# Splitting the attention output products by output rows

## The chip, the cores and the metric

The kernel runs on one core of a Trainium2 chip. The metric is the device time of one execution in microseconds. Three executions of the kernel before took 728.78, 730.17 and 731.63 us; the median is 730.17 us.

## The reference

An attention-like recurrence over 768 steps feeds two gated feed-forward stages. For 4 batches and 8 heads with a head dimension of 40:

```python
for t in range(S):
    m_new = np.maximum(f_gate[:, :, t] + m, i_gate[:, :, t])
    f_stab = np.exp(f_gate[:, :, t] + m - m_new)
    i_stab = np.exp(i_gate[:, :, t] - m_new)
    C = f_stab * C + i_stab * einsum('bhd,bhe->bhde', vt, kt)
    n = f_stab * n + i_stab * kt
    y[:, :, t] = sigmoid(o_gate_t) * (C @ qt) / max(|n . qt|, 1)
x = y.transpose(0, 2, 1, 3).reshape(3072, 320)
x = ((x @ w1) * (x @ w2)) @ w3 @ w_out
out = max(x @ v1, x @ v2, x @ v3) @ v_out
```

(The state `C`, `n` is broadcast over its two inner dimensions in the source; the lines are shortened here. The second stage's weights, which the source also calls w1 to w_out, are called v here.)

## The kernel before

**Attention in units.** The 768 steps are cut into 9 chunks: 8 of 88 steps and a last one of 64. With 4 batches and 2 groups of 4 heads that makes 72 units, numbered `u`; `ub(u)` (called at the head of each function) gives batch `b`, chunk `c`, head group `g`, the chunk's length `n` and the number `r` of rows that the products contract over (88 in the first chunk, 128 in the others, where the rows above 88 carry the state of the chunks before).

A unit has two products on TensorE. The score product (`L569` for units up to 27, four float32 products with 40 rows; `L594` for the later ones, four with 120 rows) gives `s`. VectorE multiplies it by the decay matrix `dd` into `pk` (`L610`), GpSimd writes the columns of `pk` that build the next state (`L559`). Then `outs(u)` forms the output product: for each of 4 heads, `pk` is the stationary operand and the 41 columns of `kv` (values and a column of ones) are the moving one. Its output has 128 rows: rows 0 to 87 are this chunk's outputs, the others are state for the unit `u + 2`. In the last chunk nothing follows, so there the stationary operand has only 64 columns.

`rest(u)` follows on VectorE and GpSimd: the state goes into `kv` of unit `u + 2` (`L630`), the outputs are divided by their denominators (`L643` to `L646`) and gated (`L651`). `x_cols` transposes the result (`L666`) into the feed-forward stages.

**A product in float32 is two passes.** Each `PE.matmul` on float32 operands leaves two weight loads and two matmuls in the trace: one `outs` is 4 products, or 8 passes. The products of the feed-forward stages use rounded operands (`F32R`) and are one pass each.

**Feed-forward.** `a_step` and `c_step` run groups of 8 matmuls with 128 stationary and 384 moving columns (`L698` to `L702`); `b_step` (`L765` to `L769`) and `d_step` (`L784`) accumulate; `fold` (`L926`) multiplies two weight matrices ahead of time.

**What sets the order.** A planner (`Plan.run`) simulates the engines with fixed costs and due times shifted by a table (`BIAS`) and writes out one order of instructions per engine. The cost that it is told for `outs` is a constant in the call of `P.op` (910 or 500 ns; 1210 ns together with the score product), and so the order doesn't depend on how `outs` is written. For units `u >= DUO = 28` the output product of unit `u - 1` stands in the same step as the score product of unit `u`, straight behind it. So the outputs of units 27 to 70 follow `L594`; those of units 0 to 26 and of unit 71 stand where the planner put them. Units 0 to 9 write `o` into the banks `ac0` to `ac2`, the later ones into `aq`.

Of the kernel before, what the change touches and what calls it, by code (L numbers as in the profile page):

```python
# [280 lines left out]
def mlstm_moe_kernel(  # L281
# [21 lines left out]
    V, A, G, PE, SP = nc.vector, nc.scalar, nc.gpsimd, nc.tensor, nc.sync  # L303
# [33 lines left out]
    o, where, over, gates_done = 0, {}, {t: [] for t, _ in shared}, {}  # L337
# [30 lines left out]
    def T(*key):  # L368
        return made[key]
# [7 lines left out]
    o = 0  # L377
# [30 lines left out]
    def f():  # L408
# [5 lines left out]
         r=[("g", "ff")], w=[("g", "git")])  # L414

    def f():
# [6 lines left out]
         r=[("g", "git")], w=[("g", "aug", 1)])  # L423
# [55 lines left out]
    def ub(u):  # L479
        b, r = divmod(u, 18)  # L480
        return b, r // 2, r % 2, GL[r // 2], 128 if r > 1 else L
# [41 lines left out]
    def unit(u):  # L523
# [48 lines left out]
        else:  # L572
# [19 lines left out]
            def f():  # L592
                for h in range(4):
                    PE.matmul(T("s", u)[0:L, h], lhsT=ks[:, h], rhs=T("qs", u)[:, h], start=True, stop=True)  # L594
                if duo:
                    outs(u - 1)
# [19 lines left out]
        if u + 1 < DUO or u == NU - 1:  # L616
            new(("o", u), [128, 4, 41], F32, f"ac{u % 3}" if u < 10 else "aq")
            P.op("P", 910 if m > n else 500, lambda: outs(u), cols=210, r=[("pk", u), ("kv", u)], w=[("o", u)])
            rest(u)

    def outs(u):
        b, c, g, n, r = ub(u)
        m = 128 if c < NCH - 1 else n
        for h in range(4):
            PE.matmul(T("o", u)[:m, h], lhsT=T("pk", u)[:r, h, 0:m], rhs=T("kv", u)[:r, h, 40:81], start=True, stop=True)  # L625

    def rest(u):
        b, c, g, n, r = ub(u)
# [514 lines left out]
```

## Time and profile before

| | |
|---|---|
| median of three executions | 730.17 us (728.78 to 731.63) |
| profiled execution: span from its first to its last instruction | 729.3 us (the page gives no other time for it) |
| instructions | 12666 |
| TensorE matmul (PE) busy | 699.4 us, 96%, 4341 instructions |
| TensorE weight load (PEld) busy | 674.3 us, 92%, 4341 instructions |
| VectorE (DVE) busy | 437.0 us, 60% |
| ScalarE (ACT) busy | 373.8 us, 51% |
| GpSimd (POOL) busy | 308.3 us, 42% |
| mean granted TensorE clock | 0.988 of full speed |

Matmuls are pipelined and their ends are modelled, so the time of one row is longer than the distance to the next; what TensorE really takes is read from the starts of successive rows. A row of the timeline merges neighbouring instructions of one line: start, length from the first start to the last end, and their number. `128*64` in a row is the part of the TensorE array that is used: rows times columns of the stationary operand.

### The profile page before, as it was taken

The page shows a single profiled execution, that of the slowest core. Times are in us where ns is not written, and L with a number is a line of the kernel's source. Part 1 is how long each engine was busy: PE and PEld are TensorE (multiplying, and loading weights), DVE is VectorE, ACT ScalarE, POOL GpSimd, SP SyncE. Part 2 cuts the span into 40 slices and gives each one's busy share as a digit, 9 for nine tenths or more (in the row PEclk, how much of TensorE's full clock was granted, in tenths as well). Part 3 has the DMA queues.
Part 4 walks back from the last instruction along what each step waited for, and adds up shares of the span by engine and source line. Part 5 has one row for each costly group of instructions (what it writes and reads, how often), then busy time and mean ns, then how long its engine had stood idle before and what let it go on. Part 6 is the DMA issues. An engine that isn't in the chain of part 4 may idle for free.

```text
span 729.3 us, 12666 instructions
## 1 busy us (share of the span) xinstructions
PE 699.4 (96%) x4341; PEld 674.3 (92%) x4341; DVE 437.0 (60%) x998; ACT 373.8 (51%) x697; POOL 308.3 (42%) x438
## 2 busy tenths in 40 slices
PE   1699999999999999999999999999999999999998
PEld 1677897889999999999999999999999999999998
DVE  4688876667766865866466676754747632233333
ACT  5968998689854355555343446545333222231311
POOL 1786755556646536664044456543406200000000
PEclk9978999999999999999999999999999999999999
DMA  7987887464433445543023445432305100000000
GB/s 207 251 247 226 233 230 219 146 185 157 148 88 102 117 111 148 139 124 87 12 76 85 109 121 153 113 83 69 88 1 112 49 1 27 1 1 1 1 27 28
DMA packets 50954, 78.84 MB, mean 108 GB/s; under 512 B 11882, under 2 KB 37930, under 8 KB 50890
## 3 DMA queue, kind: packets, MB, share of 16 engines
q1 hardware_dynamic: 50890, 78.04, 38.4%
q8 instruction: 34, 0.56, 0.3%
q14 instruction: 30, 0.25, 0.1%
HBM read 73.98 MB, written 4.03 MB: 107 GB/s over the span
## 4 chain that ended last, share of the span: by engine, by line
PE 84%; DMA 7%; DVE 3%; POOL 2%; issue 2%; SPq 1%; ACT 0%; POOLq 0%; DVEq 0%
PE wk L698 13%; PE wk L699 12%; PE wk L700 12%; PE ac L784 9%; PE aq L625 6%; PE wk L702 6%; PE wk L701 6%; PE ac L765 4%; PE ac L769 4%; PE wk L926 4%; PE ac L767 3%; DMA stg<-in_w3t 2%; PE aq L569 2%; PE aq L594 1%; DMA dd<-d_na 1%
## 5 line engine op out<-in xcount | busy, mean ns | idle before, releaser
L718 DVE TENSOR_TENSOR pl<-pr,ph 128x384 fp32r<-128x384 f32 (+1 forms) x91 | 60.8, 669 | 75.8 <-ACT ph L714 73.1
L714 ACT CAST ph<-pr 128x384 fp32r<-128x384 f32 (+1 forms) x114 | 57.8, 510 | 90.5 <-PE ac L784 43.9
L698 PE MATMUL wk<-xh,wch 128*128 128x384 f32 x288 | 99.5, 345 | 0.0
L700 PE MATMUL wk<-xl,wch 128*128 128x384 f32 x288 | 97.1, 337 | 0.0
L699 PE MATMUL wk<-xh,wcl 128*128 128x384 f32 x288 | 97.1, 337 | 0.0
L749 DVE TENSOR_TENSOR pr<-pr,wk 128x384 f32<-128x384 f32 (+1 forms) x98 | 52.8, 541 | 64.4 <-PE wk L702 57.8
L698 PE MATMUL wk<-xh,wah 128*128 128x384 f32 x256 | 90.9, 355 | 0.0
L718 POOL TENSOR_TENSOR pl<-pr,ph 128x384 fp32r<-128x384 f32 (+1 forms) x23 | 24.2, 1052 | 153.7 <-ACT ph L714 138.9
L699 PE MATMUL wk<-xh,wal 128*128 128x384 f32 x256 | 86.6, 338 | 0.0
L700 PE MATMUL wk<-xl,wah 128*128 128x384 f32 x256 | 86.5, 338 | 0.0
L545 POOL TENSOR_TENSOR dd<-am,dd 128x352 f32<-128x352 f32 (+2 forms) x72 | 57.5, 799 | 49.6 <-DMA dd<-d_na 48.8
L559 POOL TENSOR_TENSOR pk<-kv,dd 128x160 f32<-128x160 f32 (+1 forms) x64 | 38.7, 606 | 72.1 <-PE aq L625 64.9
L625 PE MATMUL aq<-kv,pk 128*128 128x41 f32 (+2 forms) x496 | 62.2, 275 | 2.1 <-POOL pk L559 1.4
L731 ACT COPY pr<-wk 128x384 f32<-128x384 f32 x64 | 30.5, 477 | 64.2 <-PE wk L702 64.1
L553 ACT ACTIVATE dd<-dd 128x352 f32<-128x352 f32 (+2 forms) x72 | 35.2, 492 | 52.3 <-POOL dd L549 51.7
L625 PEld LDWEIGHTS aq<-kv,pk 128*128 128x128 f32 (+2 forms) x496 | 57.4, 184 | 4.5 <-POOL pk L559 1.7
L651 POOL TENSOR_TENSOR misc<-misc 88x160 f32<-88x160 f32 (+1 forms) x62 | 41.5, 669 | 46.7 <-DVE misc L646 42.5
L746 ACT COPY pr<-wk 128x384 f32<-128x384 f32 x48 | 23.1, 482 | 70.5 <-PE wk L702 70.4
L733 DVE TENSOR_TENSOR pr<-pr,wk 128x384 f32<-128x384 f32 x64 | 35.2, 551 | 40.0 <-PE wk L702 35.7
L698 PEld LDWEIGHTS wk<-xh,wch 128*128 128x128 f32 x288 | 54.1, 188 | 0.1
L699 PEld LDWEIGHTS wk<-xh,wcl 128*128 128x128 f32 x288 | 54.2, 188 | 0.0
L700 PEld LDWEIGHTS wk<-xl,wch 128*128 128x128 f32 x288 | 54.0, 188 | 0.0
(133 smaller groups left out, 1729.5 us busy)
## 6 DMA issues: line engine op xcount, KB each, us to landing
misc<-in_qk SPq DMA_DIRECT2D x44, 330.0 KB
dd<-d_na SPq DMA_DIRECT2D x56, 176.0 KB
kv<-in_kv SPq DMA_DIRECT2D x72, 121.5 KB
stg<-in_w3t SPq DMA_DIRECT2D x13, 512.0 KB
stg<-in_wc SPq DMA_DIRECT2D x9, 512.0 KB
qq<-in_qk SPq DMA_DIRECT2D x64, 66.0 KB
misc<-in_og SPq DMA_DIRECT2D x31, 120.0 KB
out<-misc SPq DMA_DIRECT2D x23, 160.0 KB
```

The source lines that it names most:

```text
L545: P.op("G", 735, lambda: G.tensor_tensor(out=T("dd", u)[:r], in0=am[:r, c, h0:h0 + 4].unsqueeze(2).to_broadcast([r, 4, n]), in1=T("dd", u) ...
L625: PE.matmul(T("o", u)[:m, h], lhsT=T("pk", u)[:r, h, 0:m], rhs=T("kv", u)[:r, h, 40:81], start=True, stop=True)
L651: P.op("G", 485, lambda: G.tensor_tensor(out=yv(), in0=yv(), in1=sg(b, c).rearrange("p (h d) -> p h d", d=D)[:n, g * 4:g * 4 + 4], op=ALU.mult
L698: PE.matmul(p, lhsT=h_[:, kt], rhs=xh[:, kt], start=kt == 0, stop=False)
L699: PE.matmul(p, lhsT=l_[:, kt], rhs=xh[:, kt], start=False, stop=False)
L700: PE.matmul(p, lhsT=h_[:, kt], rhs=xl[:, kt], start=False, stop=False)
L701: PE.matmul(p, lhsT=r_, rhs=xh[:, 2], start=False, stop=False)
L702: PE.matmul(p, lhsT=r_, rhs=xl[:, 2], start=False, stop=True)
L714: P.op("A", act(n), lambda sl=sl: A.copy(out=T("ph", key)[:, sl], in_=T(*src)[:, sl]), r=[src + part], w=[("ph", key) + part])
L718: e.tensor_tensor(out=T("pl", key)[:, sl], in0=T(*src)[:, sl], in1=T("ph", key)[:, sl].bitcast(F32), op=ALU.subtract)
L749: P.op("V", dve(sl.stop - sl.start), lambda ps=ps, sl=sl: V.tensor_tensor(out=T(*sc)[:, sl], in0=T(*sc)[:, sl], in1=T(*ps)[:, sl], op=ALU. ...
L784: PE.matmul(T(f"ac{m}", (k, 1)), lhsT=src[:, m * 128:m * 128 + 128], rhs=w[:, o:o + DM], start=first_, stop=last_,)
```

## The change

In `outs`, each product whose stationary operand has 128 columns is written as two products of 64 columns. The first writes output rows 0 to 63, the second rows 64 to 127. Both have the same moving operand. Where the operand has 64 columns already (the last chunk), there is still one product. Nothing else changes; the planner gets the same costs, and so the order of the work is the same.

```diff
     def outs(u):
         b, c, g, n, r = ub(u)
         m = 128 if c < NCH - 1 else n
         for h in range(4):
-            PE.matmul(T("o", u)[:m, h], lhsT=T("pk", u)[:r, h, 0:m], rhs=T("kv", u)[:r, h, 40:81], start=True, stop=True)
+            for a in range(0, m, 64):
+                PE.matmul(
+                    T("o", u)[a:a + 64, h], lhsT=T("pk", u)[:r, h, a:a + 64], rhs=T("kv", u)[:r, h, 40:81],
+                    start=True, stop=True,
+                )
```

## Rows read from the trace of the kernel before

**Rows 1.** Page, busy us (share of the span) and instructions of each engine.
```profile
PE 699.4 (96%) x4341; PEld 674.3 (92%) x4341; DVE 437.0 (60%) x998; ACT 373.8 (51%) x697; POOL 308.3 (42%) x438
```

**Rows 2.** Page, the chain that ended last, share of the span by engine.
```profile
PE 84%; DMA 7%; DVE 3%; POOL 2%; issue 2%; SPq 1%; ACT 0%; POOLq 0%; DVEq 0%
```

**Rows 3.** Busy time by stretch: length, each engine's busy us (instructions), clock, DMA.
```profile
100.00:225.00 125.00, 124.22 (x755) 112.86 (x754) 86.66 (x193) 100.95 (x169) 69.51 (x89) 1.00 0.55 163
225.00:600.00 375.00, 374.33 (x2444) 371.06 (x2443) 235.50 (x566) 161.68 (x342) 170.77 (x250) 1.00 0.34 91
```

**Rows 4.** Groups by shape, L625: count, busy us, mean ns, idle before.
```profile
L625 PE MATMUL aq<-kv,pk 128*128 128x41 f32 x384 | 50.5, 281 | 2.1 <-POOL pk L559 1.4 <-DVE xl L680 0.6
...
L625 PE MATMUL aq<-kv,pk 128*64 128x41 f32 x64 | 5.3, 233 | 0.0
```

**Rows 5.** Groups by shape, weight loads of L625.
```profile
L625 PEld LDWEIGHTS aq<-kv,pk 128*128 128x128 f32 x384 | 47.3, 192 | 3.3 <-POOL pk L559 1.7 <-DVE xl L680 1.0
...
L625 PEld LDWEIGHTS aq<-kv,pk 128*64 128x64 f32 x64 | 4.3, 137 | 1.0 <-issue 0.7
```

**Rows 6.** Timeline, PE, a 128-column unit behind L594 (start us, us, what).
```profile
405.10 0.44 PE L594 MATMUL aq<-qs,kst 120*88 120x88 f32 x4
405.37 1.06 PE L625 MATMUL aq<-kv,pk 128*128 128x41 f32 x8
406.26 0.42 PE L698 MATMUL wk<-xh,wch 128*128 128x384 f32 x1
...
406.69 0.34 PE L700 MATMUL wk<-xl,wch 128*128 128x384 f32 x1
```

**Rows 7.** Timeline, PE, a 64-column unit behind L594.
```profile
435.16 0.44 PE L594 MATMUL aq<-qs,kst 120*88 120x88 f32 x4
435.53 0.66 PE L625 MATMUL aq<-kv,pk 128*64 128x41 f32 x8
436.12 0.44 PE L698 MATMUL wk<-xh,wah 128*128 128x384 f32 x1
...
436.57 0.34 PE L700 MATMUL wk<-xl,wah 128*128 128x384 f32 x1
```

**Rows 8.** Timeline, PE, a 128-column unit behind a 384-column matmul.
```profile
206.48 0.34 PE L702 MATMUL wk<-xl,wcr 128*128 128x384 f32 x1
206.65 0.98 PE L625 MATMUL aq<-kv,pk 128*128 128x41 f32 x8
207.46 0.42 PE L698 MATMUL wk<-xh,wch 128*128 128x384 f32 x1
...
207.89 0.34 PE L700 MATMUL wk<-xl,wch 128*128 128x384 f32 x1
```

**Rows 9.** Timeline, PE, a 64-column unit behind a 384-column matmul.
```profile
590.39 0.34 PE L702 MATMUL wk<-xl,war 128*128 128x384 f32 x1
590.66 0.66 PE L625 MATMUL aq<-kv,pk 128*64 128x41 f32 x8
591.25 0.45 PE L698 MATMUL wk<-xh,wah 128*128 128x384 f32 x1
...
591.71 0.34 PE L700 MATMUL wk<-xl,wah 128*128 128x384 f32 x1
```

**Rows 10.** Timeline, PE, a unit behind the 40-row score products of L569.
```profile
75.30 0.71 PE L569 MATMUL aq<-misc 40*88 40x88 f32 x7
75.94 1.09 PE L625 MATMUL aq<-kv,pk 128*128 128x41 f32 x8
```

**Rows 11.** Waits of PE: who waited for whom, us in total, times, longest.
```profile
PE aq L569 <- DMA raw<-in_qk: 10.3, 2, 8.1
...
PE aq L625 <- POOL pk L559: 1.4, 1, 1.4
```

**Rows 12.** Timeline, PE, a unit of the first 30 us.
```profile
23.87 1.93 PE L625 MATMUL ac<-kv,pk 88*128 88x41 f32 x8
25.73 2.65 PE L569 MATMUL aq<-raw 40*88 40x88 f32 x16
```

## The prediction

> **What bounds the kernel now.** I read the page's busy times first, then the chain that ended last, then busy time by stretch, then the groups by shape, and last the timeline around single units. TensorE is busy 96% of the span with matmuls and 92% with weight loads [rows 1], and 84% of the chain is its own work [rows 2]. The stretch that holds most of the changed work is fuller still: from 100 to 225 us it is busy 124.22 of 125 us, from 225 to 600 us 374.33 of 375 us [rows 3]. Nothing there waits for another engine for long, and VectorE and GpSimd have a third and more of their time free. So in these 500 us, whatever the TensorE queue gains or loses per output product, the end gains or loses. Before that TensorE waits for loads (10.3 us in two waits [rows 11]), and small delays can vanish in such waits.
>
> What bounds a single pass is read from the starts. Eight passes of 128 stationary and 41 moving columns take 1.06 us from the first start to the last end, and one is shown with 281 ns [rows 4, 6]: (1.06 - 0.28) / 7 = 111 ns per step. A unit of the last chunk has the same 41 moving columns and 64 stationary ones: (0.66 - 0.23) / 7 = 61 ns [rows 4, 7], its first, slower step included. The mean weight load is 192 ns against 137 ns, 55 ns less [rows 5], and 111 - 55 = 56. I take 58 ns. Half the stationary columns, about half the step, with the moving side unchanged: the weight load sets the pace, and the load of one pass is hidden by nothing but the matmul of the pass before.
>
> **The change part by part.** *Passes.* Of 72 units, the 8 of the last chunk stay as they are. The other 64 go from 8 passes of 128 columns to 16 of 64. If the loads of the two halves follow one another as all loads do now, that is 16 x 58 = 928 ns in place of 8 x 111 = 888 ns: 40 ns more per unit, 2.6 us in all. On passes alone it would be a change hardly to be seen.
>
> *Going in and out of the 64-column form.* The units of the last chunk are a model of what a split unit does, for they stand between the same neighbours and use 64 columns. They don't gain what their shorter steps promise. Behind `L594`, the distance from the first score pass to the third feed-forward matmul is 406.69 - 405.10 = 1.59 us with 128 columns [rows 6] and 436.57 - 435.16 = 1.41 us with 64 [rows 7]: 0.18 us saved, where 8 x 53 ns = 0.42 us should have been. The other 0.24 us stands at the two edges: 0.37 us from `L594` to the first output pass in place of 0.27, and 436.12 - 435.53 = 0.59 us until `L698` starts, where eight steps of 58 make 0.46. The same behind a 384-column matmul: 1.41 us [rows 8] against 1.32 us [rows 9], 0.09 saved of 0.42, so 0.33 us at the edges; there a load that ran under the long matmul is lost as well. These are prices of this kernel's own instructions; I take it that they hang on the 64 columns and not on the chunk.
>
> A split unit is then a last-chunk unit with eight further passes of 58 ns (0.47 us):
> - Behind `L594`: 1.41 + 0.47 - 1.59 = +0.29 us. The units are 27 to 70 without the five of the last chunk among them: 39, so +11.3 us.
> - Behind a 384- or 320-column matmul: 1.32 + 0.47 - 1.41 = +0.38 us. These are 11 of the 15 later units that remain: +4.2 us.
> - Behind the 40-row products `L569` (the other 4 of the 15, the first of them in [rows 10]): the unit there takes 1.09 us where it takes 0.98 to 1.06 elsewhere, so it pays an entry already. I charge half of the 0.24 us and the passes: +0.17 us each, +0.7 us; bounds 0.04 and 0.29.
> - The ten units of the first 60 us: here a unit takes 25.73 - 23.87 = 1.86 us [rows 12], twice what it takes later, and the neighbours are mostly 40-row products. Bounds 0 and 0.29 us each; I take 0.1, near the lower end because those edges are paid already: +1.0 us.
>
> Sum: 11.3 + 4.2 + 0.7 + 1.0 = +17.2 us.
>
> *What takes some of it back.* The output product waits for GpSimd's part of `pk` once for 1.4 us [rows 11], and twice for VectorE's `xl`, 0.6 us together [rows 4]; a later TensorE finds them shorter. I take 2.2 us off, between 0 and 4 (the two load waits stand too early for much to pile up ahead of them). That leaves +15 us.
>
> *Who waits longer.* Behind an output product stand the state for unit `u + 2` and the division on VectorE, then the gate on GpSimd. They get `o` 0.3 us later, on engines that are not full; I cost this at nothing, and if the chain from state to `pk` to output were tight, TensorE would have idle time in [rows 3]. The 512 further weight loads and matmuls write nothing extra and release nobody earlier: the signal still comes with the last pass. No DMA, no wait and no buffer is added.
>
> The profiled execution had a span of 729.3 us; it would become 744.3. The median of the runs is 0.9 us above that span, so the forecast is 745 us.
>
> **The rivals.** *The two halves load side by side (faster).* They use different columns of the array, so the load of one might run while the other's does. Then eight further passes cost nothing, and a split unit costs what a last-chunk unit costs: -0.18 us behind `L594` (39: -7.0), -0.09 behind long matmuls (11: -1.0), -0.30 behind `L569` (4: -1.2), some -0.5 early: -10 us, 720 us. It decides from the step on: the unit breaks even where 16 passes save 0.29 us, at 58 - 18 = 40 ns per pass. For it: the loads are the bound, and the columns are disjoint. Against it: every load in the trace comes one after another, and nothing before uses the upper 64 columns alone, so no row shows two at once.
> The Trainium skill speaks on both sides. "TensorEngine Tiling (Array Packing)", section Key Properties, says that different tiles of the array can load weights and multiply in parallel; by it this rival holds. "TensorE: Matmul & The Clock Gate", Part 3, The mechanism, says that a weight load overlaps with a running matmul only where the row group differs; the two halves use the same rows, so by it they would gain nothing. The trace already departs from that second rule, since loads overlap with the matmul before them on the same rows (a step of 111 ns holds both), so I don't let it decide.
>
> *Each change between the halves costs as much as an edge (much slower).* If going from rows 0-63 to rows 64-127 costs about half of 0.24 us, seven such changes stand inside each unit: 64 x 7 x 0.12 = 54 us more, 799 us. Nothing in the trace shows a change of columns within one form; the edges are seen where the form changes, and that speaks against it.
>
> *The edges don't apply.* If they belong to the last chunk and not to the 64 columns (or the halves are run in the full form), 40 ns per unit remain: +2.6 us, 733 us. Against it: the edges appear both at [rows 7] and at [rows 9], with different neighbours.
>
> **How the numbers follow.** Loads in sequence with edges: 0.54, 738 to 750 us by itself (0.20 to 0.32 us per unit behind `L594`, 0 to 4 us taken back). Halves side by side: 0.33, 717 to 729, the upper part where they overlap only in part. No edges, or an overlap near break-even: 0.07, 730 to 737. Changes between halves dear: 0.06, from 752. The range from 719 to 750 leaves out the last case and the tails. About 0.5% (3.7 us) is what a measurement can tell from no change. Faster is the rival without its upper end: 0.31. Same takes that end and the bottom of the third case: 0.07. Slower is the rest: 0.62.
>
> **What would show it.** `L625` should have 1088 passes in place of 576, all of 64 columns. A unit behind `L594` should take about 0.9 us from its first to its last start, with 58 ns per step across the change of halves too, and the entry (0.37 us) and the exit of [rows 7] on every unit. If the step across halves is near 30 ns, the first rival holds; if it is 150 ns or more at every second pass, the second. If the units are as forecast but the end moves by less than 10 us, the waits took back more than I allowed. The forecast fails altogether if the unit as a whole, entry to exit, is shorter than 1.59 us.

## The result, and the profile after

The changed kernel takes 723.39 us (median of four, 722.34 to 725.08) against 729.68 us (median of four, 728.78 to 731.63; the first three of them gave 730.17): a ratio of 0.9913, with a 95% interval of 0.9892 to 0.9934, or 6.3 us less. The time lies inside the stated range, near the first rival's 720 us. The forecast was 745 us, 15 us more than before: the direction was wrong.

In the kernel after, the line of the output products is `L626`, and the later lines are four higher (`L698` is `L702`). The page's busy times, to set beside [rows 1]:
```profile
PE 682.0 (94%) x4853; PEld 648.9 (90%) x4853; DVE 437.6 (61%) x998; ACT 373.4 (52%) x697; POOL 306.3 (42%) x438
```
TensorE has 512 more matmuls and as many more weight loads, as expected, and yet 17 us less busy time. The groups by shape say where (line, engine, operation, tiles, shape, count, busy us, mean ns); they answer to [rows 4, 5]:
```profile
L626 PE MATMUL aq<-kv,pk 128*64 128x41 f32 x832 | 37.2, 233 | 2.4 <-DVE misc L650 1.7 <-DVE xl L684 0.5
L626 PEld LDWEIGHTS aq<-kv,pk 128*64 128x64 f32 x832 | 30.6, 137 | 8.8 <-issue 2.8 <-DVE misc L650 2.0 <-DVE xl L684 1.1
```
The single pass is what the last chunk showed before: 233 ns, and 137 ns for its load. Neither got shorter. But 832 loads of 137 ns are busy for 30.6 us, where 64 such loads took 4.3 us. In sequence 832 would have taken 13 times that, 56 us. Busy time counts a moment once however many loads run in it, and 30.6 us is about what 448 loads take in sequence: the 64 of the last chunk and half of the other 768. So one of every two of these ran beside another.

The timeline of one unit, behind `L594` (start us, us, what), for [rows 6]:
```profile
402.55 0.44 PE L594 MATMUL aq<-qs,kst 120*88 120x88 f32 x4
402.92 0.67 PE L626 MATMUL aq<-kv,pk 128*64 128x41 f32 x16
403.51 0.44 PE L702 MATMUL wk<-xh,wch 128*128 128x384 f32 x1
...
403.96 0.33 PE L704 MATMUL wk<-xl,wch 128*128 128x384 f32 x1
```
Sixteen passes take 0.67 us; the eight of a last-chunk unit took 0.66 [rows 7]. From the first score pass to the third feed-forward matmul it is 1.41 us, the last chunk's value, in place of 1.59. How two passes start is seen in a stretch of 40 ns that ends just behind the first start, in this unit and in a last-chunk unit of the same kernel:
```profile
402.92 0.26 PE L626 MATMUL aq<-kv,pk 128*64 128x41 f32 x2
...
428.62 0.25 PE L626 MATMUL aq<-kv,pk 128*64 128x41 f32 x1
```
Two have started in the split unit, one in the other. In the trace the starts of the split unit lie 7 and 51 ns apart in turn (one step of 58 ns for both halves), those of the last chunk 58 ns. The form and the length of each pass are the same in both; what differs is that the split unit has passes for the other 64 columns (and so for the other output rows: the two go together in every kernel here, and no run separates them).

Behind a 384-column matmul, for [rows 8]:
```profile
206.70 0.34 PE L706 MATMUL wk<-xl,wcr 128*128 128x384 f32 x1
206.97 0.67 PE L626 MATMUL aq<-kv,pk 128*64 128x41 f32 x16
207.56 0.45 PE L702 MATMUL wk<-xh,wch 128*128 128x384 f32 x1
...
208.02 0.33 PE L704 MATMUL wk<-xl,wch 128*128 128x384 f32 x1
```
1.32 us in place of 1.41, again the value that the last chunk had before [rows 9]. Behind `L569`, the unit of [rows 10] took 76.85 - 75.94 = 0.91 us until `L698` started; the passes now take 78.69 - 78.09 = 0.60 us until `L702` starts. The row of before, then those of after:
```profile
76.85 0.42 PE L698 MATMUL wk<-xh,wah 128*128 128x384 f32 x1
```
```profile
78.09 0.67 PE L626 MATMUL aq<-kv,pk 128*64 128x41 f32 x16
78.69 0.44 PE L702 MATMUL wk<-xh,wah 128*128 128x384 f32 x1
```

From the division of unit 9 (the last early one) to that of unit 71 took 591.36 - 62.08 = 529.28 us before and takes 585.18 - 64.22 = 520.96 us after, 8.3 us less. The rows of before, then those of after:
```profile
62.08 0.15 DVE L643 TENSOR_SCALAR rd<-ac 88x4 f32<-88x4 f32 x1
...
591.36 0.15 DVE L643 TENSOR_SCALAR rd<-aq 64x4 f32<-64x4 f32 x1
```
```profile
64.22 0.15 DVE L647 TENSOR_SCALAR rd<-ac 88x4 f32<-88x4 f32 x1
...
585.18 0.15 DVE L647 TENSOR_SCALAR rd<-aq 64x4 f32<-64x4 f32 x1
```
So this execution lost 2.1 us before unit 9 and gained 8.3 us behind it. In the early part the shorter products became waits (us in total, times, longest). The first answers to [rows 11]; the second was 1.0 us before (the single row), and the third is not in the list of before:
```profile
PE aq L666 <- DVE pk L610: 1.0, 1, 1.0
```
```profile
PE aq L569 <- DMA raw<-in_qk: 11.6, 3, 8.1
...
PE aq L670 <- DVE pk L610: 4.4, 2, 3.3
PE ac L626 <- DVE kv L634: 4.1, 2, 2.1
```

### The profile page after: what moved, and what is told of

Read it like the earlier page. It is cut to its first block, busy times and chain, and to the rows that moved or that the text cites. A ratio compares the mean times of both kernels' runs of the same rounds, so it can differ in the third digit from the quotient of the medians.

```text
span 723.1 us, 13690 instructions
## 1 busy us (share of the span) xinstructions
PE 682.0 (94%) x4853; PEld 648.9 (90%) x4853; DVE 437.6 (61%) x998; ACT 373.4 (52%) x697; POOL 306.3 (42%) x438
## 4 chain that ended last, share of the span: by engine, by line
PE 78%; ACT 7%; DMA 6%; DVE 3%; issue 2%; POOL 2%; SPq 1%; POOLq 0%; DVEq 0%
PE wk L702 13%; PE wk L704 11%; PE wk L703 11%; PE ac L788 9%; PE wk L706 6%; PE wk L705 6%; PE ac L769 4%; PE aq L626 4%; PE ac L773 4%; PE ac L771 3%; PE wk L930 2%; ACT stg L874 2%; PE aq L594 1%; PE aq L569 1%; DMA qq<-in_qk 1%
## 5 line engine op out<-in xcount | busy, mean ns | idle before, releaser
L702 PE MATMUL wk<-xh,wch 128*128 128x384 f32 x288 | 99.7, 346 | 0.0
L702 PE MATMUL wk<-xh,wah 128*128 128x384 f32 x256 | 90.8, 355 | 0.0
L545 POOL TENSOR_TENSOR dd<-am,dd 128x352 f32<-128x352 f32 (+2 forms) x72 | 55.9, 777 | 54.7 <-DMA dd<-d_na 54.0
L655 POOL TENSOR_TENSOR misc<-misc 88x160 f32<-88x160 f32 (+1 forms) x62 | 44.4, 715 | 41.6 <-DVE misc L650 37.8
L874 ACT ACTIVATE stg<-stg 128x512 f16<-128x512 f32 (+2 forms) x41 | 52.7, 1285 | 4.5 <-DVE stg L866 4.0
L702 PEld LDWEIGHTS wk<-xh,wch 128*128 128x128 f32 x288 | 54.1, 188 | 1.0
L788 PE MATMUL ac<-wd,ph 128*128 128x320 f32 x288 | 51.4, 313 | 0.0
```

The source lines that it names most:

```text
L545: P.op("G", 735, lambda: G.tensor_tensor(out=T("dd", u)[:r], in0=am[:r, c, h0:h0 + 4].unsqueeze(2).to_broadcast([r, 4, n]), in1=T("dd", u) ...
L655: P.op("G", 485, lambda: G.tensor_tensor(out=yv(), in0=yv(), in1=sg(b, c).rearrange("p (h d) -> p h d", d=D)[:n, g * 4:g * 4 + 4], op=ALU.mult
L702: PE.matmul(p, lhsT=h_[:, kt], rhs=xh[:, kt], start=kt == 0, stop=False)
L788: PE.matmul(T(f"ac{m}", (k, 1)), lhsT=src[:, m * 128:m * 128 + 128], rhs=w[:, o:o + DM], start=first_, stop=last_,)
L874: A.activation(out=sign, in_=tl()[:, :, 1].bitcast(F32), func=AF.Copy)
```

## The experiments

The theory after the result: passes that use different columns of the array load and multiply side by side, and the cost of going in and out of the 64-column form is paid as forecast. The rival to it: the gain comes from something else in the split (cheaper edges, or the early part), and the two halves run together only by accident of their order.

**The changed kernel again**, unaltered:

> The changed kernel unaltered, beside the others on the same chip: 722 to 725 us by every theory.

723.0 us (ratio 0.9916, 0.9888 to 0.9944).

**Halves as the outer loop.**
```diff
-        for h in range(4):
-            for a in range(0, m, 64):
+        for a in range(0, m, 64):
+            for h in range(4):
```


> The same 64-column products, but the halves are the outer loop: four heads write rows 0 to 63, then four heads rows 64 to 127. Theory A (halves run side by side only if they are neighbours in the program): there is one neighbouring pair per unit, the other passes step by 58 ns, and the whole is what was forecast for loads in sequence, 743 to 747 us. Theory B (each half of the columns takes its own next pass, whatever stands between in the program): the pairs 7 ns apart remain, and it takes what the split kernel takes, 722 to 725 us.

735.46 us, ratio 1.0079 (1.0048 to 1.0110): neither theory. The same 16 passes in another order make the kernel slower than before. A unit behind `L594`:
```profile
367.82 0.44 PE L594 MATMUL aq<-qs,kst 120*88 120x88 f32 x4
368.19 0.92 PE L626 MATMUL aq<-kv,pk 128*64 128x41 f32 x16
...
369.49 0.33 PE L704 MATMUL wk<-xl,wch 128*128 128x384 f32 x1
```
0.92 us in place of 0.67: (0.92 - 0.23) / 58 ns is 12 steps, where full overlap takes 8 and none 16. Two stretches that begin just ahead of the first pass, of 0.26 and 0.30 us, tell when the second half begins:
```profile
368.19 0.43 PE L626 MATMUL aq<-kv,pk 128*64 128x41 f32 x4
...
368.19 0.51 PE L626 MATMUL aq<-kv,pk 128*64 128x41 f32 x6
```
Four passes of the first half start alone; the fifth has a second one 6 ns behind it. At that time three passes of the first half still wait. From there on both halves run beside each other, until the last four of the second half stand alone. So TensorE does look past waiting passes for one whose columns are free, but not past any number. Four further steps of 58 ns in 54 units are 12.5 us, and this kernel is 735.46 - 723.0 = 12.5 us slower than the split one: the gain comes from the passes that run beside each other, and not from the narrower form.

**Halves of two heads at a time**, made to test that number.
```diff
-        for h in range(4):
+        for p in range(0, 4, 2):
             for a in range(0, m, 64):
+                for h in range(p, p + 2):
```


> The order of the split products within a unit: rows 0 to 63 of two heads, then rows 64 to 127 of the same two, then the other two heads. In the trace with the halves as the outer loop the second half began when three passes of the first were still waiting, not when four or more were. Theory A (TensorE looks past up to three waiting passes): here three wait in front of the second half's first pass, so the pairs 7 ns apart begin at once and it takes what the split kernel takes, 722 to 725 us. Theory B (it looks past one product, two passes, at most): the second half begins a step of 58 ns or more late twice per unit, 54 x 0.12 = 6 us more, 728 to 731 us.

724.56 us, ratio 0.9918 (0.9891 to 0.9946): theory A. Three passes of the first half wait in front of the second half's first, and it starts at once: the stretch of 30 ns behind the first start holds two (first row). In the trace the second lies 13 ns behind the first, not 7, and later pairs up to 27 ns apart, but the unit still takes eight steps. That four waiting passes are too many is read from the order by halves alone. The unit takes 250.87 - 249.43 = 1.44 us against 1.41:
```profile
249.81 0.26 PE L627 MATMUL aq<-kv,pk 128*64 128x41 f32 x2
```
```profile
249.43 0.44 PE L594 MATMUL aq<-qs,kst 120*88 120x88 f32 x4
249.81 0.69 PE L627 MATMUL aq<-kv,pk 128*64 128x41 f32 x16
...
250.87 0.33 PE L705 MATMUL wk<-xl,wch 128*128 128x384 f32 x1
```

**One head of four split**, to weigh the edges by themselves.
```diff
-            for a in range(0, m, 64):
+            w = 64 if h == 3 else m
+            for a in range(0, m, w):
```
(with `w` in place of 64 in the slices)

> Only the product of the last head of each unit is split; the other three have 128 columns. If going into and out of the 64-column form costs 0.24 us whatever stands inside: each unit pays it and gains two steps of 53 ns, +0.13 us on 54 units: +7 us, 735 to 738 us. If the edges cost nothing and the split gains in proportion: a quarter of the split kernel's gain, 728 us.

736.63 us, ratio 1.0100 (1.0071 to 1.0128), +6.9 us: the edges are paid, whole, for one split product as for four. A unit, 369.49 - 367.74 = 1.75 us in place of 1.59:
```profile
367.74 0.44 PE L594 MATMUL aq<-qs,kst 120*88 120x88 f32 x4
368.01 1.09 PE L627 MATMUL aq<-kv,pk 128*128 128x41 f32 x10
...
369.49 0.34 PE L705 MATMUL wk<-xl,wch 128*128 128x384 f32 x1
```

**Quarters.**
```diff
-            for a in range(0, m, 64):
+            for a in range(0, m, 32):
```
(with 32 in the slices; the last chunk is then split too)

> Four products of 32 output rows instead of two of 64 (the last chunk: two of 32 instead of one of 64). Side by side without limit: a step of four passes is set by the shorter load or the matmul and falls from 58 to some 37 to 40 ns; a unit gains 8 x 0.02 = 0.16 us more over the split kernel, 72 units: about 11 us, 711 to 715 us. Only two at a time: the 32 passes go in 16 steps of 31 to 37 ns, as long as now or longer: 722 to 730 us. In sequence: 32 x 31 ns, 0.5 us more per unit: 750 us or more.

714.72 us, ratio 0.9796 (0.9771 to 0.9821), and 714.58 us (0.9776 to 0.9803) when run again: the first theory, four at a time. Four passes have started within 30 ns of the first (first row), and 32 passes take 0.51 us; the unit takes 358.37 - 357.11 = 1.26 us:
```profile
357.48 0.24 PE L626 MATMUL aq<-kv,pk 128*32 128x41 f32 x4
```
```profile
357.11 0.44 PE L594 MATMUL aq<-qs,kst 120*88 120x88 f32 x4
357.48 0.51 PE L626 MATMUL aq<-kv,pk 128*32 128x41 f32 x32
...
358.37 0.34 PE L704 MATMUL wk<-xl,wch 128*128 128x384 f32 x1
```


> Products of 32 output rows in all units, unaltered, beside the others on the same chip: 713.5 to 715.5 us by both theories.

**The early units apart.**
```diff
-            for a in range(0, m, 64):
+            w = 64 if u >= 10 else m
+            for a in range(0, m, w):
```
(`u < 10` in the second, 32 in place of 64 in the third)

> Only units 10 to 71 are split; the ten units of the first 60 us keep 128 columns. In the two traces the end of a unit moves by -8.4 us between unit 9 and unit 71. Theory A (the early units lose some 2 us when split, since their gain turns into waits and their loads shift): 720.5 to 722 us, 1 to 2 us below the fully split kernel. Theory B (the early difference is only scatter between runs): the same as the fully split kernel, 722.5 to 723.5 us.

722.22 us, ratio 0.9895 (0.9880 to 0.9910).

> Only units 0 to 9 are split. Theory A: 731 to 732 us, 1 to 2 us above the kernel before. Theory B: 729 to 730 us, the same as before. If those units were bound by TensorE as the later ones are: 726 us.

729.97 us, ratio 1.0010 (0.9996 to 1.0024).

> Products of 32 output rows in units 10 to 71 only. In the trace of the kernel with quarters everywhere the ends move by -17.9 us from unit 9 to unit 71. Theory A: 711 to 713 us. Theory B: as with quarters everywhere, 714 to 715 us.

713.32 us, ratio 0.9777 (0.9764 to 0.9790): the fastest version found, 16.4 us below the kernel before.

The early units are not bound by TensorE: splitting them gains nothing. Whether it costs something stays open. Both kernels that leave them whole are about 1 us below the ones that split them (722.22 against 723.0 and 723.39, 713.32 against 714.58), but their intervals overlap, and the interval of the early split alone holds no change. Single executions differ by more there: the division of unit 9 came at 64.22 us in one trace of the split kernel and at 62.56 in the other.

## Why the prediction was wrong

*What bounds the kernel* was right. From 100 to 600 us TensorE stays full, and nearly all of what a unit gains behind unit 9 arrives at the end. Priced by the rows: 39 x 0.18 + 11 x 0.09 + 4 x 0.3 = 9.2 us; 8.3 us came in the trace. TensorE's idle time from 100 to 600 us grew from 1.45 us [rows 3] to 1.07 + 1.60 = 2.67 us, which is about the part that is missing:
```profile
100.00:225.00 125.00, 123.93 (x854) 109.62 (x853) 91.02 (x195) 102.66 (x172) 70.50 (x92) 1.00 0.57 165
225.00:600.00 375.00, 373.40 (x2793) 365.96 (x2792) 236.82 (x570) 163.91 (x346) 173.21 (x251) 1.00 0.36 91
```

*The passes* are the step that failed: "If the loads of the two halves follow one another as all loads do now, that is 16 x 58 = 928 ns". The 58 ns were right and the 16 was wrong: 16 passes take eight steps, 0.47 us less per unit than I charged. The forecast for a unit was 1.41 + 0.47 us and the measured unit 1.41, below the 1.59 us that the prediction had named as the sign of its failure. That is the first rival's term, to the last digit; I gave it 0.33.

The error lay in how I weighed the evidence. "Every load in the trace comes one after another" was true, but every one of them needed columns that the load before it used too. No row could have shown two at once, and so the rows spoke neither for nor against the rival; I took them as speaking against it. The last chunk was a fair model of the form and said nothing about two column ranges.

The Trainium skill had both answers, and I let neither decide. "TensorEngine Tiling (Array Packing)", section Key Properties, has different tiles load weights and multiply in parallel: the runs agree, with 7 ns between the two halves' starts. "TensorE: Matmul & The Clock Gate", Part 3, The mechanism, has a load overlap with a running matmul only in another row group: here the halves use the same rows, and it overlaps all the same, by the same 7 ns.

*The edges* were right. 0.24 us per unit was read off the last chunk, and the experiment with one head pays it with only two steps of 53 ns in return: +6.9 us for a forecast of +7. "The edges don't apply" falls with it. Without them a split unit would be 0.24 us shorter still. The Trainium skill's "TensorEngine Tiling (Array Packing)", section Key Properties, has a change of tiling mode drain TensorE; the later start of the first pass (0.37 us behind `L594` in place of 0.27) agrees.

*Changes between halves* cost nothing: halves alternate at every pass, and a unit is no longer than one that never changes.

*The early units* were charged +1.0 us, and the rival credited them with -0.5. They gain nothing, and may lose up to some 1 us. In the two profiled executions the early part lost 2.1 us in place of the rival's 0.5 gained, and the later units gained 8.3 us in place of 9.2: together 3.5 us, the distance from 720 to 723.4 us. How much of the 2.1 us is the split's and how much scatter stays open.

The prediction saw that a unit takes twice as long there and gave no cause. The rows show one for part of that stretch: from 46 to 58 us the granted clock is 0.50 of full speed (1.2 GHz), before and after the change. A unit in it takes 53.85 - 52.09 = 1.76 us before and 54.95 - 53.94 = 1.01 us after. The split is worth more there than later, and still nothing is gained: TensorE only waits longer, busy 10.98 of these 12 us before and 8.62 after. It had been busy 13.67 (before) and 9.60 (after) of the 15 us from 30 to 45 us, and from 60 to 80 us the clock is 1.00 in both. The rows of before, then those of after:
```profile
46.00:58.00 12.00, 10.98 (x48) 9.37 (x49) 10.53 (x30) 7.96 (x12) 8.89 (x14) 0.50 0.89 260
52.09 1.83 PE L625 MATMUL ac<-kv,pk 128*128 128x41 f32 x8
53.85 1.47 PE L569 MATMUL aq<-raw 40*88 40x88 f32 x8
```
```profile
46.00:58.00 12.00, 8.62 (x62) 7.21 (x63) 9.17 (x29) 7.81 (x13) 7.81 (x13) 0.50 0.86 245
53.94 1.08 PE L626 MATMUL ac<-kv,pk 128*64 128x41 f32 x16
54.95 1.33 PE L569 MATMUL aq<-raw 40*88 40x88 f32 x7
```

*What takes some of it back* had its sign from the same step: a later TensorE was to find shorter waits (-2.2 us). It came earlier, and waits grew.

*Who waits longer* did not come into it, since `o` came earlier, not later.

## What to carry to other kernels

Where TensorE is what the kernel waits for, a short product whose pace is set by its weight load gets faster when its stationary operand is split over separate columns, as long as the gain (here eight steps of 111 ns that become eight of 58, 0.42 us per unit) is more than the price of entering and leaving the narrower form (0.24 to 0.33 us here); with a single product it is not. Passes on different columns should stand near each other in the program: with three passes of the same half between them the gain was kept, and the same 16 passes, sorted by half, lost all of it. And where a trace cannot show a thing because nothing in it could have caused it, its absence is no evidence.

## What was not expected of the hardware

- Two passes on different columns start 7 ns apart, and four on quarters of the array within 30 ns, on the same rows and with the same moving data.
- TensorE starts a pass on free columns past three waiting passes; in the order by halves, with seven in front of it at first, it began only when three were left.
- With quarters the step of four passes is 36 ns in the trace. The load alone would allow less: 64 columns take 58 ns and 128 take 111, so each column adds 0.83 ns and 32 come to some 31 ns by estimate. The matmul of 41 columns may be what is left; no run separates the two.
